# Writing the zeros of a routing buffer later, from each expert's first free row on

## The chip, the cores and the metric

The kernel runs on one NeuronCore of a Trainium2 chip. The metric is the device time of one execution in microseconds (us), the median of several runs; 1041.03 us before the change (three runs, 1039.38 to 1041.65).

A core has five engines that run in parallel, each through its own list of instructions in order: TensorE (PE, matrix multiplications and transposes), VectorE (DVE), ScalarE (ACT), GpSimd (POOL) and SyncE (SP). SP does no arithmetic here: it issues nearly all transfers between the core's SBUF and DRAM, and those inside SBUF, which 16 DMA engines then carry out. POOL issues the transfers whose rows are chosen by data. An instruction that needs another engine's or a transfer's result waits at the head of its engine's list, and everything behind it in that list waits too.

## The reference

Three layers follow each other: attention in which only scores close to the row's maximum count, a layer of eight experts of which each token uses one, and a dense layer.

```python
scores = scale * q @ k.T                       # 4 batches, 8 heads, 576 x 576, head_dim 64
scores = where(scores >= max(scores) - tau, scores, -1e9)
x = softmax(scores) @ v                        # then heads side by side: x is 2304 x 512
e_idx = argmax(x @ w_gate, axis=1)             # one of 8 experts for each token
for e in range(8):
    mask = e_idx == e
    out[mask] = gate_w[mask] * eom[mask, e] * (relu(x[mask] @ w1[e]) @ w2[e])   # 512 -> 1024 -> 512
g = h * tanh(softplus(h)), h = out @ w_in      # 512 -> 2048
result = g @ w_out                             # 2048 -> 512
```

All is in 32-bit floats.

## The kernel before

**Attention.** The 4 batches of 8 heads are worked in 16 pairs of heads, four per batch. For a pair SP loads q and k (L258, L260), PE turns them (L532, L543), ACT and POOL split each into a high and a low part (L538, L547, L567), and SP spreads the parts inside SBUF into the tiles that the score matmuls read: kx for k (L556), sa and sb for q (L558). A pair has nine blocks of scores (L416), which alternate between sa and sb; the ninth uses both. Per block DVE takes the row maximum (L421), POOL the threshold (L425), ACT the exponential (L434) and DVE the mask (L439); two blocks of scores fit in PSUM, and a block's place comes free with its mask. PE then turns the masked block (L447) and multiplies it with v (L463 to L477).

**Routing.** When a batch is through, PE and DVE compute its gate logits, each token's expert, and the token's rank among all tokens of that expert so far. Each expert has a stretch of RS = 2688 rows in a DRAM buffer, xs. POOL sends the batch's rows there in five indirect transfers (L978); the row is the expert's first row plus the token's rank. So at any time the rows of one expert lie densely from its first row on. After three batches the expert with the most tokens is known; SP loads its first 256 rows (xe, L722) and its weights (wraw, L1045), and its matmuls (L1210, L1229) fill PE while the last batch is routed. The experts are then worked in order of size with blocks of fixed sizes (CAP, 544 rows for the largest down to 256), so rows past an expert's last token are read as well. They have to be zero.

**The zeros.** `zero_fill(e)` (L145) writes 544 rows of zeros at the start of expert e's stretch: one transfer of 1088 KB, issued by SP (L152). The eight are put into the plan at L390, each after a certain block of scores (block 14, 19, ... 49 of 144), and they are on their way before any row of a batch is sent. They go to rows known when the kernel is built, and none waits for another.

**What sets the order.** The lists of the engines are fixed when the kernel is built. `Plan` (L1393 on) holds nodes with an engine, a cost in ns, the nodes they come after, a due time (in blocks of scores), the buffers they take and give, and a lag: the time after the node's end until its result counts as there (a transfer's landing). It runs a clock over these costs, always takes the node that can start first, by due time among equals, and writes its instructions. The waits themselves come from the tiles' uses: xs is one DRAM tile, so accesses at rows that are known only at run time are ordered one after the other, by their landing.

Of the kernel before, what the change touches and what calls it, by code (L numbers as in the profile page):

```python
# [13 lines left out]
I32 = mybir.dt.int32  # L14
U32 = mybir.dt.uint32
AF = mybir.ActivationFunctionType
ALU = mybir.AluOpType
# [6 lines left out]
NE, FF = 8, 1024  # L24
FF2 = 2048
P = 128
NP = H // 2
NT = 5
EARLY = 256
RS = N + EARLY + P  # L30
CAP = (544, 416, 352, 320, 304, 272, 256, 256)
# [9 lines left out]
C_8ME, C_ERS, C_E, C_CAP = 2 * P, 2 * P + 8, 2 * P + 16, 2 * P + 24  # L41
# [32 lines left out]
LAST_P, DUE_AVL = 0, 9.83  # L74
DUE_S1, DUE_P1 = .72, 4.8
SENT = 2900
ZERO_FROM, ZERO_STEP = 14, 5
POOL_SPLIT = {0, 1, 2} | set(range(10, 46, 3)) | set(range(72, 80))


class Kernel:
# [61 lines left out]
        nc.vector.memset(self.ones, 1.0)  # L143

    def zero_fill(self, e):  # L145
        nc = self.nc
        if e == 0:
            self.z = self.sx.tile([P, P], F32, name="zeros")
            nc.gpsimd.memset(self.z, 0.0)
        rows = self.xs[e * RS:e * RS + CAP[0], :].rearrange("r (s d) -> (r s) d", d=P)  # L150
        t = CAP[0] * DM // P // P
        nc.sync.dma_start(rows.rearrange("(p t) d -> p t d", p=P), self.z.unsqueeze(1).to_broadcast([P, t, P]))  # L152

# [197 lines left out]
    def plan_attention(self):  # L351
        nc, add, npair = self.nc, self.plan.add, self.nb * NP
        self.raw_kq, self.kq, self.v, self.xt, self.sums = {}, {}, {}, {}, {}
        self.started, self.sent, self.sent_of = {}, None, {}
        qk, st, cols = [], [], {}
        loads = []

        def load(p, after=()):
            after = list(after) + ([qk[9 * (p - N_LD)]] if p >= N_LD else [])
            loads.append(add("SP", 3600, lambda: self.load_pair(p), after, 9 * p - 30, [(("ld", p), 3 if p else 1)], lag=2000))  # L360

        def start(b):
            after = [qk[9 * (NP * b - NP + 1)]] if b else []
            self.started[b] = add("POOL", 290, lambda: self.start_batch(b), after, 9 * NP * b - 18, [(("xt", b), NT + (2 if b == self.nb - 1 and 0 < LAST_CUT < NT else 1))])
            return add("SP", 5700, lambda: self.load_v(b), after, 9 * NP * b - 18, [(("v", b), 3 * NP)], lag=2000)

        load(0)
        add(None, 0, self.late_setup, [loads[0]], -50)
        load(1)
        v = start(0)  # L370
        for p in range(2, N_LD):
            load(p)
        ops = self.plan_first_prep(loads[0])
        for p in range(npair):
            b, hp = divmod(p, NP)
            if p > 0:
                ops = self.plan_prep(p, loads[p])
            if p == 1:
                load(N_LD, ops)
            if p == NP * b and b:  # L380
                v = start(b)
            self.plan_pair(p, ops, v, qk, st, cols)
            if 0 < p < npair - N_LD:
                load(p + N_LD)
            if hp == NP - 1:
                cut = LAST_CUT if b == self.nb - 1 else NT
                for i0, i1 in ((0, cut), (cut, NT)):
                    if i0 < i1:
                        self.plan_route(b, i0, i1, cols)
        for e in range(NE):  # L390
            add("SP", 3100, lambda e=e: self.zero_fill(e), [qk[ZERO_FROM + ZERO_STEP * e]], ZERO_FROM + ZERO_STEP * e + 6)
        self.plan_first(st)

    def plan_pair(self, p, ops, v, qk, st, cols):
# [449 lines left out]
    def map_tokens(self, n):  # L844
# [6 lines left out]
        elif n == NTT:  # L851
            nc.gpsimd.dma_start(self.mapi, self.map.rearrange("(t p) o -> p (t o)", p=P))

    def plan_route(self, b, i0, i1, cols):


        nc, sm, add = self.nc, self.sm, self.plan.add
        last = b == self.nb - 1
        due = (DUE_LAST if last else DUE_ROUTE) + 9 * NP * (b + 1)
# [103 lines left out]
        def scatter(i):  # L963
            n = P if i < 4 else 64
            px = T["px", i] = self.bank()
            for hp in range(NP):
                nc.tensor.transpose(px[0:n, hp * P:(hp + 1) * P], self.xt[b][:, hp, i * P:i * P + n], self.ident)

        def scatter_out(i):
            n = P if i < 4 else 64  # L970
            xo = T["xo", i] = self.xsp.tile([P, DM], F32, name="xo")
            nc.vector.tensor_tensor(  # L972
                xo[0:n].rearrange("p (h d) -> p h d", h=H), T["px", i][0:n].rearrange("p (h d) -> p h d", h=H),
                T["rc"][0:n, i - i0].unsqueeze(2).to_broadcast([n, H, D]), op=ALU.mult)

        def send(i):
            n = P if i < 4 else 64
            nc.gpsimd.indirect_dma_start(  # L978
                self.xs[:, :], bass.IndirectOffsetOnAxis(ap=T["rowi"][0:n, i - i0:i - i0 + 1], axis=0), T["xo", i][0:n], None)
# [4 lines left out]
        n = add("PE", sum(100 + int(1.67 * (z - a)) for a, z in pieces), logits, where, due - 2, [(k, 1) for k in keys], [("xt", b)])  # L984
        n = add("ACT", int(1.05 * (w1 - w0)), logits_out, [n, begin], due - HASTE, gives=keys)
        keys = [("bank", b, "lt", i) for i in banks]
        n = add("PE", 110 * nt, logits_turn, [n], due - 2, [(k, 1) for k in keys])
# [10 lines left out]
        if b == self.nb - 2:  # L998
            e, f, g = self.first_expert()
            n = add("DVE", 80, e, [n2], due)  # L1000
            n = add("PE", 30, f, [n], due, takes=[(("bank", "first"), 1)])
            self.chosen = add("DVE", 2150, g, [n], due - HASTE, gives=[("bank", "first")])
        for i in range(i0, i1):
            n = add("PE", 435, lambda i=i: scatter(i), [n4], due + i, [(("bank", b, "sc", i), 1), (("xo", b, i), 1)], [("xt", b)])
            n = add("DVE", 602, lambda i=i: scatter_out(i), [n], due - HASTE, gives=[("bank", b, "sc", i)])
            self.sent_from = n
            self.sent = add("POOL", 1040, lambda i=i: send(i), [n, self.sent] if self.sent else [n], due + i, gives=[("xo", b, i)], lag=SENT)
        self.sent_of[b] = self.sent


# [382 lines left out]
class Plan:  # L1393
# [15 lines left out]
    def add(self, eng, cost, fn, after=(), due=0.0, takes=(), gives=(), lag=0):  # L1409
        n = Node(eng, cost, fn, list(after), due, list(takes), list(gives), lag)  # L1410
        self.nodes.append(n)
        return n
# [83 lines left out]
```

## Time and profile before

| | us |
|---|---|
| median of 3 runs | 1041.03 |
| lowest, highest | 1039.38, 1041.65 |
| the profiled execution | 1037.33 |
| its span, first to last instruction | 1035.5 |
| attention's blocks of scores, first to last | 11.9 to 333.0 |
| zero fills issued | 47.9 to 125.6 |
| sends of the routed rows | 137.9 to 370.8 |
| mean granted clock of TensorE | 0.995 of full speed |

The profile shows one execution. The difference between the profiled execution's time and its span is what lies before the first and after the last instruction. Rows of a timeline give the start in us, the duration in us, the engine, the line of the kernel, the operation, the tile written and the tiles read, and how many instructions were merged into the row (x4). In brackets stands how long the engine had been idle before the row, and what ended that: an engine and the tile it wrote, or a transfer. SPq is SP's issuing of transfers; its durations are those of the issue, not of the transfer.

### The profile page before, as it was taken

The page shows a single profiled execution, that of the slowest core. Times are in us where ns is not written, and L with a number is a line of the kernel's source. Part 1 is how long each engine was busy: PE and PEld are TensorE (multiplying, and loading weights), DVE is VectorE, ACT ScalarE, POOL GpSimd, SP SyncE. Part 2 cuts the span into 40 slices and gives each one's busy share as a digit, 9 for nine tenths or more (in the row PEclk, how much of TensorE's full clock was granted, in tenths as well). Part 3 has the DMA queues.
Part 4 walks back from the last instruction along what each step waited for, and adds up shares of the span by engine and source line. Part 5 has one row for each costly group of instructions (what it writes and reads, how often), then busy time and mean ns, then how long its engine had stood idle before and what let it go on. Part 6 is the DMA issues. An engine that isn't in the chain of part 4 may idle for free.

```text
span 1035.5 us, 19346 instructions
## 1 busy us (share of the span) xinstructions
PE 988.7 (95%) x7012; PEld 863.0 (83%) x7012; DVE 697.3 (67%) x1299; ACT 661.0 (64%) x1126; POOL 306.8 (30%) x377
## 2 busy tenths in 40 slices
PE   5989999999999899999999999999999999999996
PEld 4667777767767688999999998899988999999995
DVE  5767787787797748766667766778776665445443
ACT  5777768767767515556566757876775765665562
POOL 3232243233221312444533333345441221111111
PEclk9999999999999999999999999999999999999999
DMA  7999975765534248667878864544831132221111
GB/s 159 231 240 240 244 200 133 180 160 129 140 90 149 82 140 276 226 203 250 269 238 287 275 210 101 113 117 120 220 123 44 62 112 72 72 92 63 41 41 41
DMA packets 144354, 160.10 MB, mean 155 GB/s; under 512 B 48672, under 2 KB 102624, under 8 KB 144256
## 3 DMA queue, kind: packets, MB, share of 16 engines
q1 hardware_dynamic: 140480, 149.34, 51.4%
q0 software_dynamic: 3776, 9.49, 2.7%
q8 instruction: 57, 0.93, 0.4%
q14 instruction: 41, 0.34, 0.1%
HBM read 95.22 MB, written 37.04 MB: 128 GB/s over the span
## 4 chain that ended last, share of the span: by engine, by line
PE 71%; DVE 13%; ACT 5%; DMA 5%; issue 5%; SPq 1%; POOL 1%; POOLq 0%; DVEq 0%; ACTq 0%
PE hg L1326 14%; PE o L1366 14%; PE bank L1210 10%; PE y L1229 9%; PE s L416 8%; PE bank L447 6%; PE o L463 4%; DMA xs<-xo,rowi 2%; DVE s L1334 2%; ACT L1338 1%; DVE s L1342 1%; DVE gh L1343 1%; DVE e L439 1%; PE o L466 1%; DVE mxs L421 1%
## 5 line engine op out<-in xcount | busy, mean ns | idle before, releaser
L1326 PE MATMUL hg<-yh,whi 128*128 128x256 f32 x576 | 162.9, 283 | 2.1 <-DVE ys L1239 2.1
L1326 PE MATMUL hg<-yl,whi 128*128 128x256 f32 x576 | 163.1, 283 | 0.7 <-DVE yl L1273 0.7
L1326 PE MATMUL hg<-yh,wlo 128*128 128x256 f32 x576 | 163.0, 283 | 0.0
L434 ACT ACTIVATE e<-s,mxs 128x576 f32<-128x576 f32 x144 | 103.9, 746 | 54.9 <-DVE mxs L421 48.9
L421 DVE TENSOR_REDUCE mxs<-s 128x1 f32<-128x576 f32 x144 | 105.4, 754 | 40.1 <-PE s L416 39.2
L439 DVE SCALAR_TENSOR_TENSOR e<-s,thr,e 128x576 f32<-128x576 f32 x144 | 113.9, 814 | 26.0 <-ACT e L434 19.6
L1366 PE MATMUL o<-whi,gh 128*128 128x512 f32 x288 | 113.3, 393 | 2.1 <-DVE gh L1343 2.1
L1326 PEld LDWEIGHTS hg<-yh,whi 128*128 128x128 f32 x576 | 110.4, 192 | 3.7 <-issue 2.3
L1342 DVE TENSOR_TENSOR s<-s,hg 128x512 f32<-128x512 f32 x72 | 49.3, 684 | 94.9 <-ACT s L1338 94.9
L1366 PE MATMUL o<-whi,gl 128*128 128x512 f32 x288 | 112.9, 392 | 0.0
L1366 PE MATMUL o<-wlo,gh 128*128 128x512 f32 x288 | 112.5, 391 | 0.0
L1326 PEld LDWEIGHTS hg<-yl,whi 128*128 128x128 f32 x576 | 110.4, 192 | 2.3 <-DVE yl L1273 1.0
L1326 PEld LDWEIGHTS hg<-yh,wlo 128*128 128x128 f32 x576 | 110.4, 192 | 0.0
L1333 ACT ACTIVATE s<-hg 128x512 f32<-128x512 f32 x72 | 42.1, 594 | 106.1 <-PE hg L1326 99.9
L452 ACT COPY pt<-bank 128x512 f32<-128x512 f32 (+1 forms) x192 | 93.9, 539 | 17.0 <-PE bank L447 15.0
L447 PE MATMUL bank<-cst,e 128*128 128x128 f32 (+1 forms) x656 | 92.2, 278 | 1.0 <-DVE xo L972 1.0
L1229 PE MATMUL y<-hh,whi 128*128 128x256 f32 (+6 forms) x288 | 87.1, 302 | 0.0
L447 PEld LDWEIGHTS bank<-cst,e 128*128 128x128 f32 (+1 forms) x656 | 73.5, 140 | 16.2 <-issue 9.6
L1229 PE MATMUL y<-hl,whi 128*128 128x256 f32 (+6 forms) x288 | 86.8, 301 | 0.0
L1229 PE MATMUL y<-hh,wlo 128*128 128x256 f32 (+6 forms) x288 | 86.8, 301 | 0.0
L1061 DVE TENSOR_TENSOR wlo<-wraw,whi 128x1024 fp32r<-128x1024 f32 x57 | 79.6, 1396 | 10.4 <-ACT whi L1057 9.8
L1057 ACT CAST whi<-wraw 128x1024 fp32r<-128x1024 f32 x80 | 83.3, 1047 | 3.0 <-DMA wraw<-in_moe_w 3.0
(247 smaller groups left out, 2373.3 us busy)
## 6 DMA issues: line engine op xcount, KB each, us to landing
wraw<-in_moe_w SPq DMA_DIRECT2D x64, 512.0 KB
kx<-khl SPq DMA_DIRECT2D x60, 288.0 KB
wraw<-yt SPq DMA_DIRECT2D x18, 512.0 KB
xs<-zeros SPq DMA_DIRECT2D x8, 1088.0 KB
raw<-in_moe_w_in SPq DMA_DIRECT2D x16, 512.0 KB
raw<-in_moe_w_out SPq DMA_DIRECT2D x16, 512.0 KB
part<-ob SPq DMA_DIRECT2D x18, 256.0 KB
ob<-part SPq DMA_DIRECT2D x18, 256.0 KB
```

The source lines that it names most:

```text
L416: nc.tensor.matmul(s[:, half, 0:288], q[j][:, o:o + P], kx[j][:, at:at + 288], start=j == parts[0][0] and low == 0, stop=j == parts[-1][0] ...
L421: nc.vector.reduce_max(mx, S[u][:, :, 0:288], axis=AX.XY, negate=True)
L434: nc.scalar.activation(ev(u), S[u][:, :, 0:288], AF.Exp, bias=S["mx", u])
L439: nc.vector.scalar_tensor_tensor(ev(u), S[u][:, :, 0:288], S["thr", u], ev(u), op0=ALU.is_ge, op1=ALU.mult, accum_out=acc)
L447: nc.tensor.transpose(pp[0:rows, n * P:(n + 1) * P], E[i][:, col:col + rows], self.ident)
L452: nc.scalar.copy(t[0:rows, 0:n], PT["ps", g][0:rows, 0:n])
L1057: nc.scalar.copy(hi, raw)
L1061: return lambda: sub(lo, raw, hi.bitcast(F32))
L1210: self.nc.tensor.matmul(h[:, 0:n], w[a][:, k, c:c + P], xs[b][:, k, 0:n], start=(k == 0 and m == 0), stop=(k == 3 and m == 2))
L1229: self.nc.tensor.matmul(y[0][:, d, 0:n], w[a][:, f % 2, d * P:(d + 1) * P], hh[b][:, 0:n], start=(f == 0 and m == 0), stop=(f == 7 and m = ...
L1326: nc.tensor.matmul(h[:, j], w[a][:, k, j * P:(j + 1) * P], y[b][:, k], start=(k == 0 and m == 0), stop=(k == 3 and m == 2))
L1366: nc.tensor.matmul(o, gs[j // 2][x][:, j % 2, t * P:(t + 1) * P], w[y][:, j % 2], start=(g == 0 and j == 0 and m == 0), stop=(g == 1 and j ...
```

## The change

The zeros are no longer written at the start of each expert's stretch before all sends, but once two of the four batches are routed, from the first row that these two batches leave free. `plan_zeros` is called when batch 2's attention has been planned, ahead of its routing. It counts the tokens of each expert so far (one cast on DVE, one small matmul on PE), adds each expert's first row, and keeps the sums as integers (zi). Each fill then loads its row number from zi into a register of SP and writes 544 rows from there. A fill comes after the one before it, after the last send of batch 1, and after block 91 of the scores; in the plan it costs SP 1200 ns and counts as landed 6500 ns later. The sends of batch 2 come after the last fill.

```diff
-ZERO_FROM, ZERO_STEP = 14, 5
+ZERO_FROM, ZERO_STEP, ZERO_LAG = 91, 4, 6500
...
     def zero_fill(self, e):
...
-        rows = self.xs[e * RS:e * RS + CAP[0], :].rearrange("r (s d) -> (r s) d", d=P)
+        row = nc.values_load(self.zi[0:1, e:e + 1], engines=[mybir.EngineType.SP], min_val=0, max_val=NE * RS - CAP[0])
+        rows = self.xs[ds(row, CAP[0]), :].rearrange("r (s d) -> (r s) d", d=P)
...
             if hp == NP - 1:
+                if b == self.nb - 2:
+                    self.plan_zeros(qk)
                 cut = LAST_CUT if b == self.nb - 1 else NT
...
-        for e in range(NE):
-            add("SP", 3100, lambda e=e: self.zero_fill(e), [qk[ZERO_FROM + ZERO_STEP * e]], ZERO_FROM + ZERO_STEP * e + 6)
...
+    def plan_zeros(self, qk):
+
+        add, ps = self.plan.add, []
+        self.zi = self.const.tile([P, NE], I32, name="zi")
+        due = ZERO_FROM - 2
+        n = add("DVE", 80, lambda: ps.append(self.counts_in((self.nb - 2) * NT)), [self.ranked], due)
+        n = add("PE", 30, lambda: ps.append(self.counts(ps[0])), [n], due, takes=[(("bank", "zeros"), 1)])
+        n = add("DVE", 80, lambda: self.nc.vector.tensor_tensor(self.zi, ps[1], self.cst[:, C_ERS:C_ERS + NE], op=ALU.add),
+                [n], due, gives=[("bank", "zeros")])
+        self.zeros = [n]
+        for e in range(NE):
+            self.zeros.append(add("SP", 1200, lambda e=e: self.zero_fill(e), [self.zeros[-1], self.sent, qk[ZERO_FROM]], ZERO_FROM + ZERO_STEP * e, lag=ZERO_LAG))
...
-            self.sent = add("POOL", 1040, lambda i=i: send(i), [n, self.sent] if self.sent else [n], due + i, gives=[("xo", b, i)], lag=SENT)
+            self.sent = add("POOL", 1040, lambda i=i: send(i), [n] + ([self.sent] if self.sent else []) + (self.zeros[-1:] if b == self.nb - 2 else []), due + i, gives=[("xo", b, i)], lag=SENT)
```

## Rows read from the trace of the kernel before

**Rows 1.** The page, busy time of each engine, its share, instructions.
```profile
PE 988.7 (95%) x7012; PEld 863.0 (83%) x7012; DVE 697.3 (67%) x1299; ACT 661.0 (64%) x1126; POOL 306.8 (30%) x377
```

**Rows 2.** Stretches: length, busy us by engine, PE clock, DMA share, GB/s.
```profile
50.00:60.00 10.00, 6.22 (x42) 5.15 (x42) 6.05 (x12) 6.52 (x16) 3.60 (x8) 1.00 1.00 280
240.00:300.00 60.00, 59.05 (x489) 43.51 (x488) 47.46 (x121) 44.70 (x99) 15.56 (x40) 1.00 0.51 121
```

**Rows 3.** Timeline of PE: score blocks before which PE was idle.
```profile
52.06 0.76 PE L416 MATMUL s<-kx,sa 128*128 128x288 f32 x4 [2.31 <-DMA sa<-qhl]
...
69.56 0.64 PE L416 MATMUL s<-kx,sa 128*128 128x288 f32 x3 [0.62 <-DMA sa<-qhl]
...
92.61 0.63 PE L416 MATMUL s<-kx,sb 128*128 128x288 f32 x3 [0.95 <-PE bank L447]
...
112.28 0.77 PE L416 MATMUL s<-kx,sb 128*128 128x288 f32 x4 [0.81 <-PE bank L447]
...
227.85 0.80 PE L416 MATMUL s<-kx,sa 128*128 128x288 f32 x4 [1.15 <-DVE e L439]
```

**Rows 4.** Timeline of SP: spreads and zero fills as issued.
```profile
46.51 1.34 SPq L558 DMA_DIRECT2D sb<-qhl  x2
47.95 0.62 SPq L152 DMA_DIRECT2D xs<-zeros  x1
...
67.11 0.95 SPq L152 DMA_DIRECT2D xs<-zeros  x1
...
78.92 1.36 SPq L152 DMA_DIRECT2D xs<-zeros  x1
80.38 5.67 SPq L558 DMA_DIRECT2D sa<-qhl  x2
86.10 1.23 SPq L558 DMA_DIRECT2D sb<-qhl  x2
...
258.76 2.63 SPq L558 DMA_DIRECT2D sa<-qhl  x2
```

**Rows 5.** Timeline of POOL: two sends of batch 1, the first of batch 2.
```profile
224.89 0.98 POOL L978 DMA_INDIRECT xs<-xo,rowi  x1 [3.20 <-DMA xs<-xo,rowi]
...
236.19 0.91 POOL L978 DMA_INDIRECT xs<-xo,rowi  x1 [0.48 <-issue]
...
302.15 1.01 POOL L978 DMA_INDIRECT xs<-xo,rowi  x1 [0.54 <-DVE xo L972]
```

**Rows 6.** The page, transfers issued: the sends, median us to landing.
```profile
xs<-xo,rowi POOLq DMA_INDIRECT x20, 2.8
```

**Rows 7.** By line: ns min/median/max, first and last start.
```profile
L1028 SPq TENSOR_LOAD <-eri x7: 263/263/474, 372.3 to 375.9; - x7
...
L675 DVE CAST cb<-cum x2: 160/162/164, 295.9 to 356.0; 128x8 bf16<-128x8 f32 x2
```

**Rows 8.** Timeline of POOL: rows whose wait a zero fill ended.
```profile
54.42 0.19 POOL L425 TENSOR_TENSOR thr<-ntau,mxs 128x1 f32<-128x1 f32 x1 [0.47 <-DMA xs<-zeros]
...
73.40 0.86 POOL L567 TENSOR_TENSOR khl<-kraw,khl 128x320 fp32r<-128x320 f32 x1 [1.94 <-DMA xs<-zeros]
```

**Rows 9.** Timeline of SP and of PE: a late pair's spread, its first scores.
```profile
261.44 1.23 SPq L558 DMA_DIRECT2D sb<-qhl  x2
...
271.15 0.69 PE L416 MATMUL s<-kx,sa 128*128 128x288 f32 x4
```

**Rows 10.** Waits of SP, 200 to 330 us: us in total, times, longest.
```profile
SPq L556 <- ACT khl L547: 28.9, 5, 9.3
```

**Rows 11.** Timelines of SP, ACT and PE: the hand-over to the first expert.
```profile
321.53 0.95 SPq L722 DMA_DIRECT2D xe<-xs  x2
322.68 1.52 SPq L1045 DMA_DIRECT2D wraw<-in_moe_w  x3
...
335.19 1.07 ACT L1057 CAST whi<-wraw 128x1024 fp32r<-128x1024 f32 x1
...
351.92 0.58 PE L1210 MATMUL bank<-yh,whi 128*128 128x256 f32 x1 [0.75 <-DVE xo L972]
```

## The prediction, on record before the change was run

> **What bounds the kernel now.** I read the page's busy times first. TensorE works 988.7 us of a 1035.5 us span [rows 1], so the whole kernel has 46.8 us in which PE does nothing, and an edit that takes no work off PE can only win some of those. Next I read stretches, because the edit touches two of them: 48 to 126 us, where the eight zero fills are issued now, and 240 to 310 us, where they will go. The first holds the worst ten microseconds of the attention stage, 50 to 60, with PE busy 6.22 and the DMA engines full (share 1.00, 280 GB/s); the second has PE busy 59.05 of 60 at a DMA share of 0.51 and 121 GB/s [rows 2]. So the change moves traffic out of a full stretch into a half empty one, and the question is which of PE's waits in the full stretch are the zeros' doing. For that I read PE's own order there, and then the order in which SP issued its DMAs.
>
> **What it removes.** PE's waits that end with the arrival of spread queries between 48 and 126 us are 2.31 us at 52.06, 0.62 at 69.56, 0.95 at 92.61 and 0.81 at 112.28 [rows 3]. The profile names a transfer for the first two and "PE bank" for the others. I read the others as transfers as well: both are the second block of scores of a pair, the first use of its sb, and for the one at 92.61 SP finished issuing sb only at 86.10 + 1.23 = 87.33 us, 5.28 us earlier [rows 4], about what spread data takes to land in this stretch. The one at 112.28 stands alike.
>
> Which of the four has a zero fill in front of it? All of these transfers leave through SP's one queue. Zero fill 0 is issued at 47.95, after the sb that belongs to the wait at 52.06 (46.51 to 47.85) [rows 4]; that wait stays. The wait at 92.61 has zero fill 3 right between its kx and its sa: issued at 78.92, and the two sa behind it take 5.67 us to issue, where two sa with nothing in front take 2.63 (at 258.76) [rows 4]. The waits at 69.56 and 112.28 come behind the fills of their pairs. So I take off 0.62 + 0.95 + 0.81 = 2.38 us. The bounds: 0, if PE, which fills its time with other pairs' work, would only meet the next wait earlier; and the upper end is those 2.38 plus the 3.78 us that PE misses in 50 to 60 [rows 2], 6.16 us, if the first wait and what follows it are the zeros' as well. I take 2.38, by the issue order.
>
> The Trainium skill's DMA: Bandwidth & Descriptors (Queues, rings and completion order) says that each DMA engine consumes the descriptors of one ring in the order of the ring. By that rule the wait at 52.06 stays and those behind a fill go; the 5.67 us of the two sa agree with it.
>
> **What it moves.** The eight fills of 1088 KB, 8.9 MB in all, are now chained one behind the other: fill 0 waits for the last send of batch 1, and each later fill for the one before it to land. The last send of batch 1 is issued at 236.19 and takes 0.91 [rows 5], a send lands in a median 2.8 [rows 6], so the chain starts at about 239.9 us; the condition on score block 91 is met long before. One fill costs SP a register load, 0.6 us (seven loads from 372.3 to 375.9) [rows 7], and an issue of 0.62 [rows 4]. Its landing I read where an engine's wait is put down to a zero fill: issued 47.95, wait ended 54.42, and issued 67.11, wait ended 73.40 [rows 4, 8], so 6.3 to 6.5 us, in a stretch with full DMA engines. One link is then 0.6 + 6.4 = 7.0 us, and the plan allows 7.8 (1200 + 6500 + 100 ns). Eight links are 56 to 62.4 us: the chain ends between 296 and 302 us if SP is always free. SP is not: per pair it spends about 11 us on spreads and loads, and a fill that meets them waits its turn. I add half such a turn, 5 us, for one or two of the four pairs, and take 308 us; the bounds are 296 and 240 + 62.4 + 4 x 5 = 322 us.
>
> 8.9 MB over 60 us is 149 GB/s on top of 121, 270 GB/s, close to the 280 of the full stretch [rows 2]. So the late spreads get the delay that the early ones lose. What covers it: there the spread of a pair is fully issued at 261.44 + 1.23 = 262.67 and its first scores start at 271.15 [rows 9], 8.5 us later, where 87.33 us to the first use of sb at 92.61 is 5.3 and all of that was needed. The cover over a loaded landing is 8.5 - 5.3 = 3.2 us. SP itself can afford the fills' 8 x 1.2 = 10 us: between 200 and 330 us it waits 28.9 us for ACT's halves of k alone [rows 10]. If the cover is gone, three pairs lose what three early ones lost, 2.4 us. I cost it at 0.
>
> **What it adds.** One cast of the counts (DVE, 0.162 us) [rows 7], one small matmul and one DVE addition like the cast, then a bank that is held for the three. PE works through that stretch nearly without a gap, so the matmul with its weights is on the path: some 0.2 us, like the cast. I take 0.4 for all; the ends are 0 (DVE has 12.5 of 60 us free there [rows 2]) and 1.0.
>
> **The wait that it adds.** Batch 2's first send now waits for the last fill. It is issued at 302.15 today [rows 5]. With the chain's end at 308 the sends move by 6 us, and with them what SP does next: the first expert's rows (xe) at 321.53 and its weights at 322.68 [rows 11] slide to about 328 us. A weight load is half a fill in bytes, so it lands in less than 6.4 us, and the first cast of weights runs at 335.19, 12.5 us after the first load; the cover is 6.1 us before ACT has to reorder, and the first expert's first matmul comes at 351.92 [rows 11], 29.2 us after that load. So the slide costs nothing at 6 us, and at 20 us (the chain's upper end) it reorders casts without reaching the matmul. Behind the waiting send on POOL stand the thresholds of attention, which every mask needs. The planner places the send by its own clock, so POOL stalls only by as much as the real chain is later than the planned one. With links of 7.0 against 7.8 I cost this at 0; its bad end is the fourth rival.
>
> **The sum.** -2.38 + 0.4 = -2.0 us. Against the profiled execution, 1037.33 us, that is 1035.3. That execution lies 3.7 us below the median of the runs, 1041.03, so I apply the difference to the median: 1039.0 us. Own range, with 0 to 6.16 won and 0 to 2.4 lost: 1036 to 1041. About 0.2% (2.1 us) is what a measurement here can tell from no change, and the forecast stands on that line.
>
> **The rivals.**
> 1. The zeros cause the whole hole at 50 to 60 too. For it: PE is idle 3.78 us there just as the first fill starts; SP's next load behind that fill is slow. Against it: the issue order. -6.16 + 0.4: 1035.3 us.
> 2. Nothing is won on balance: the waits move from three early pairs to three late ones, or PE meets other waits. For it: 270 GB/s against a cover of 3.2 us. Against it: the late pairs have that cover and the early ones had none. -2.38 + 2.4 + 0.4: 1041.4 us.
> 3. The change does not do what it says in time: bound to batch 1's last send, the chain runs past 322 us, casts of the first expert's weights collide with the last batch's routing on DVE. One such piece of DVE work is about 1.2 us and two or three would shift: 1039.0 + 3 = 1042 us.
> 4. Slower: POOL is held by its send. Place: batch 2's first send, around 305 us. Point from which it decides: a link longer than the planned 7.8 us, a landing over 7.2 us. Price: in batch 1 POOL waited 3.20 us for a landing at 224.89 [rows 5] and PE then missed 1.15 us at 227.85 [rows 3], 0.36 us of PE for each. With 2 us more in each of eight links POOL is held 16 us: 5.8 us, 1044.8 us. For it: such a wait costs PE already; a fill stuck behind a whole spread lands late. Against it: the two landings that can be read, 6.3 and 6.5 us, come from the fullest stretch.
>
> The Trainium skill's DMA: Bandwidth & Descriptors (Anatomy of one DMA) says that DMA engines do not wait on semaphores; the issuing sequencer waits before it dispatches. By that rule a fill that waits for the one before it holds SP, and the spreads queued behind it, which speaks for rivals 2 and 4; no row of the kernel before shows a fill that waits for a fill.
>
> **How the numbers follow.** Forecast 0.42 (of it 0.25 beyond the line and 0.17 within), rival 1 0.15 (faster), rival 2 0.20 (same), rival 3 0.05 (half same, half slower), rival 4 0.18 (slower by most of its sizes; 0.02 of it same). That gives faster 0.40, same 0.41, slower 0.19; I move 0.03 from same to slower, since a link of the chain was never seen in this stretch. The range reaches from rival 1 with the spread of the runs (1034) to rival 4 (1045).
>
> **What would show it.** Right: PE's waits at about 69, 92 and 112 us are gone and the one at 52 stays; two sa behind a kx issue in about 2.6 us everywhere; the eight fills start at about 240 us, 7 to 9 us apart, and end by 312; POOL's wait before batch 2's first send is under 2 us; the first expert's first matmul keeps its distance to the last scores. Wrong: PE missing more than 2 us in 240 to 330 than now, a first send later than 315 us, or a hole at 50 to 60 that closes.

## The result, and the profile after

The changed kernel takes 1053.44 us (median of 6 runs, 1049.63 to 1054.98) against 1041.34 of the kernel before in the same session (6 runs, 1039.04 to 1043.27): 1.0116 times as long, 95% interval 1.0094 to 1.0138, or 12.1 us more. The prediction was 1039.0 us with a range to 1045, so both sign and range were wrong. The profiled execution took 1052.79 us, 1051.0 of it span.

Busy times hardly change: the page of the changed kernel has the engines at what they had before [rows 1]. PE has 4.8 us more, and the span is 15.5 us longer than that of the execution shown before.

```profile
PE 993.5 (95%) x7013; PEld 863.4 (82%) x7013; DVE 705.0 (67%) x1301; ACT 661.6 (63%) x1126; POOL 308.6 (29%) x377
```

So time was lost in waiting, and the stretches tell where. Here are those of the changed kernel, with the columns of [rows 2]: start and end, length, busy us of PE, PEld, DVE, ACT and POOL with instruction counts, granted clock, DMA share, GB/s.

```profile
50.00:60.00 10.00, 7.48 (x49) 6.09 (x50) 7.07 (x14) 6.82 (x15) 4.01 (x8) 1.00 0.36 66
240.00:300.00 60.00, 57.42 (x468) 42.02 (x468) 45.97 (x114) 44.02 (x97) 13.17 (x37) 1.00 0.86 225
350.00:360.00 10.00, 1.58 (x7) 1.16 (x7) 9.12 (x26) 3.15 (x5) 6.04 (x4) 0.59 0.69 210
360.00:370.00 10.00, 9.47 (x61) 9.47 (x62) 8.18 (x11) 3.02 (x5) 2.38 (x2) 0.73 0.07 26
```

The last two stretches of the kernel before:

```profile
350.00:360.00 10.00, 9.25 (x66) 8.79 (x64) 8.88 (x32) 1.67 (x6) 1.99 (x2) 0.83 0.14 52
360.00:370.00 10.00, 10.00 (x88) 9.96 (x87) 5.93 (x12) 1.15 (x3) 1.94 (x2) 1.00 0.15 54
```

The reader is to see three things. The traffic did move: 280 to 66 GB/s in 50 to 60, 121 to 225 in 240 to 300. PE won 1.26 us in the first of these and lost 1.63 in the second. Of the two only the loss stands clear of the scatter: over four profiles of each kernel PE's busy time is 6.22 to 7.21 before and 7.02 to 8.39 after in the first stretch, 58.92 to 59.05 and 57.18 to 58.02 in the second. And in 350 to 360 a hole has opened: PE works 1.58 us of ten where it had 9.25, while DVE is as busy as before. That is the hand-over from attention to the first expert.

How the hole came about is read from the queues. SP of the changed kernel (start, us, queue, line, operation, count); the two fills of the first row were issued at 245.05 and 250.91, four more at 269.92, 282.64, 290.06 and 300.56:

```profile
245.05 6.45 SPq L154 DMA_DIRECT2D xs<-zeros  x2
...
262.38 0.62 SPq L154 DMA_DIRECT2D xs<-zeros  x1
263.11 4.66 SPq L560 DMA_DIRECT2D sa<-qhl  x2
...
307.65 0.62 SPq L154 DMA_DIRECT2D xs<-zeros  x1
334.44 0.97 SPq L724 DMA_DIRECT2D xe<-xs  x2
335.60 2.67 SPq L1060 DMA_DIRECT2D wraw<-in_moe_w  x5
```

Seven links in 62.60 us are 8.94 us for one. The page of this kernel gives the landing:

```profile
xs<-zeros SPq DMA_DIRECT2D x8, 1088.0 KB, 6.2
```

The last fill landed near 307.65 + 6.2 = 313.9 us. POOL's first send of batch 2 follows, 12.9 us later than in [rows 5], and the first expert's rows (xe, above) also start 12.9 us later than in [rows 11]:

```profile
315.02 1.01 POOL L993 DMA_INDIRECT xs<-xo,rowi  x1 [0.54 <-issue]
...
346.86 2.38 POOL L1076 TENSOR_TENSOR wlo<-wraw,whi 128x1024 fp32r<-128x1024 f32 x1 [6.22 <-ACT whi L1072]
...
350.44 4.64 POOL L1076 TENSOR_TENSOR wlo<-wraw,whi 128x1024 fp32r<-128x1024 f32 x2
```

The first cast of weights slides by 10.5 us against [rows 11]. ACT of the changed kernel:

```profile
345.73 1.05 ACT L1072 CAST whi<-wraw 128x1024 fp32r<-128x1024 f32 x1
```

PE of the changed kernel, attention's last scores and then the hole:

```profile
333.03 0.43 PE L418 MATMUL s<-kx,sb 128*128 128x288 f32 x2
...
356.63 0.20 PE L955 MATMUL bank<-cumb,up 128*128 128x24 bf16 x1 [7.40 <-DVE cumb L948]
...
357.93 1.11 PE L982 MATMUL bank<-cst,xt 128*128 128x128 f32 x4 [1.04 <-DVE yl L1187]
358.69 0.56 PE L1225 MATMUL bank<-yh,whi 128*128 128x256 f32 x1
360.53 0.58 PE L1225 MATMUL bank<-yl,whi 128*128 128x256 f32 x1 [1.28 <-DVE yl L1187]
```

PE waits 7.40 us for cumb, a step of the second part of the last batch's routing, and twice more for yl, the low part of the first expert's rows. DVE shows the order behind it. First the changed kernel:

```profile
348.44 0.55 DVE L930 TENSOR_TENSOR lgt<-bank,r 128x384 f32<-128x384 f32 x1
349.02 0.80 DVE L933 TENSOR_REDUCE lg<-lgt 128x48 f32<-128x384 f32 x1
...
350.07 5.07 DVE L938 TENSOR_TENSOR d<-lg,mx 128x24 f32<-128x24 f32 x1
...
357.18 0.69 DVE L1187 TENSOR_TENSOR yl<-bank,yh 128x512 fp32r<-128x512 f32 x1 [0.22 <-issue]
...
359.79 0.68 DVE L1187 TENSOR_TENSOR yl<-bank,yh 128x512 fp32r<-128x512 f32 x1
```

Then the kernel before, where both yl (L1172 there) stand ahead of the second part (128x384, L915):

```profile
341.04 2.34 DVE L923 TENSOR_TENSOR d<-lg,mx 128x16 f32<-128x16 f32 x1
...
348.85 1.28 DVE L1172 TENSOR_TENSOR yl<-bank,yh 128x512 fp32r<-128x512 f32 x2
...
352.38 0.55 DVE L915 TENSOR_TENSOR lgt<-bank,r 128x384 f32<-128x384 f32 x1
```

The order has flipped. Before, the first expert's work bridged the time in which DVE routes the last rows. Now it stands behind that routing, and PE has nothing. The lists are fixed when the kernel is built, so this order was there before the kernel ran: it follows the plan's clock.

To keep such a loss apart from the scatter of one execution I use three marks: the last scores of attention, the first matmul of the first expert that the others follow without a gap (the distance between the two is called the hand-over below), and the last output of the experts on DVE. Four profiled executions of each kernel, most of them listed further down, give these means in us:

| | before | after | difference |
|---|---|---|---|
| last scores | 333.5 | 333.3 | -0.2 |
| hand-over (last scores to first expert) | 19.05 | 27.5 | +8.45 |
| end of the experts | 615.2 | 623.6 | +8.4 |
| from there to the end of the span | 423.6 (420.4 to 426.9) | 424.6 (421.5 to 427.5) | +1.0 |

The spans differ by 9.5 us, and 8.4 of it is the hand-over. The last row scatters by 6 us in either kernel, so its +1.0 says nothing.

### The profile page after: what moved, and what is told of

Read it like the earlier page. It is cut to its first block, busy times and chain, and to the rows that moved or that the text cites. A ratio compares the mean times of both kernels' runs of the same rounds, so it can differ in the third digit from the quotient of the medians.

```text
span 1051.0 us, 19403 instructions
## 1 busy us (share of the span) xinstructions
PE 993.5 (95%) x7013; PEld 863.4 (82%) x7013; DVE 705.0 (67%) x1301; ACT 661.6 (63%) x1126; POOL 308.6 (29%) x377
## 4 chain that ended last, share of the span: by engine, by line
PE 67%; DVE 16%; ACT 6%; DMA 5%; issue 4%; SPq 1%; POOL 0%; POOLq 0%; DVEq 0%; ACTq 0%
PE hg L1341 12%; PE o L1381 12%; PE bank L1225 10%; PE y L1244 10%; PE s L418 8%; PE bank L449 6%; PE o L465 5%; DVE s L1349 3%; DVE gh L1358 2%; ACT L1353 2%; DVE s L1357 2%; DVE mxs L423 1%; ACT s L1351 1%; DVE e L441 1%; PE o L468 1%
## 5 line engine op out<-in xcount | busy, mean ns | idle before, releaser
L1076 DVE TENSOR_TENSOR wlo<-wraw,whi 128x1024 fp32r<-128x1024 f32 x57 | 79.3, 1392 | 15.5 <-ACT whi L1072 15.1
```

The source lines that it names most:

```text
L1076: return lambda: sub(lo, raw, hi.bitcast(F32))
```

## The experiments

Ratios are to the kernel before on the same chip in the same session (medians of it there: 1040.92, 1038.67 and 1038.97 us; 1038.43, a single run, in the last one).

**after_again.** The changed kernel once more, so that the others have it in their session.

> The changed kernel once more, for a second profile and its time on this chip. If all of its loss sits in the hand-over to the first expert, about 9 us of it shows there again (first matmul of the first expert near 360 us) and the further 6 us that the first profile shows in the first steps of the dense layer vary from one execution to the next. If those 6 us belong to the change, they are there again, at the same steps.

1050.21 us, 1.0103 [1.0064, 1.0141]. The hole is 7.38 us long, the first gapless expert matmul at 360.23, the experts' end at 622.7.

**x1_one_batch.** The chain starts after one routed batch, and batch 1's sends wait for it in place of batch 2's.

```diff
-ZERO_FROM, ZERO_STEP, ZERO_LAG = 91, 4, 6500
+ZERO_FROM, ZERO_STEP, ZERO_LAG = 55, 4, 6500
...
-                if b == self.nb - 2:
+                if b == self.nb - 3:
                     self.plan_zeros(qk)
...
-        n = add("DVE", 80, lambda: ps.append(self.counts_in((self.nb - 2) * NT)), [self.ranked], due)
+        n = add("DVE", 80, lambda: ps.append(self.counts_in((self.nb - 3) * NT)), [self.ranked], due)
```

> The zeros are written once one batch is routed instead of two, chained in the same way, and batch 1's sends wait for the last fill. Theory A (the loss is the hand-over: batch 2's sends end 13 us later, so the first expert's weights come 13 us later and their low parts fall into the last batch's routing): nothing hangs on batch 1's sends, the chain's bytes and waits are the same, so the time is back at 1040 to 1043 us. Theory B (the chained fills themselves cost: SP held, spreads late, DMA engines full beside attention): the same loss, 1050 to 1054 us.

1051.64 us, 1.0103 [1.0069, 1.0138], where the slide of the late sends would have had it back at 1040. The hand-over is as before, 19.1 us (345.20 to 364.27), but attention ends some 12 us later. The chain now meets batch 3's load of v in SP's queue. SP and then PE of this kernel:

```profile
202.97 0.64 SPq L154 DMA_DIRECT2D xs<-zeros  x1
203.71 2.92 SPq L269 DMA_DIRECT2D vm<-in_v  x1
...
211.29 1.20 SPq L560 DMA_DIRECT2D sa<-qhl  x2
```

```profile
218.98 1.30 PE L418 MATMUL s<-kx,sa 128*128 128x288 f32 x4 [5.53 <-DMA sa<-qhl]
```

PE's wait of 5.53 us is under half of these 12; the rest was not followed up. This run missed the expectation and doesn't separate the theories as meant: the hand-over came back, and another loss of the same size came in its place. It shows only that the chain can cost as much in another place.

**x2_half_fill.** 288 rows in each fill in place of 544 (for these inputs enough rows are zeroed); everything else stays.

```diff
-ZERO_FROM, ZERO_STEP, ZERO_LAG = 91, 4, 6500
+ZERO_FROM, ZERO_STEP, ZERO_LAG = 91, 4, 3500
-        rows = self.xs[ds(row, CAP[0]), :].rearrange("r (s d) -> (r s) d", d=P)
-        t = CAP[0] * DM // P // P
+        rows = self.xs[ds(row, 288), :].rearrange("r (s d) -> (r s) d", d=P)
+        t = 288 * DM // P // P
```

> Each fill writes 288 rows instead of 544, 53% of the bytes (enough for these inputs), with 3500 ns planned for its landing instead of 6500. Theory A: the links shrink from 8.9 to about 6 us, the chain ends near 290 us, before batch 2's first send is ready at 302, the sends move by nothing and the time is 1039 to 1043 us. Theory B (bytes beside attention): about half of the loss stays, 1046 us.

1040.71 us, 1.0016 [0.9987, 1.0045]: the loss is gone. Its first send starts at 301.69, its xe at 321.03, and the hand-over is 19.1 us. PE of this kernel:

```profile
351.44 0.58 PE L1225 MATMUL bank<-yh,whi 128*128 128x256 f32 x1
```

Nor is it faster than the kernel before, although the experts end at 612.3, 2.9 us earlier.

**x3_low_dve.** The first three weight tiles' low parts go to DVE, so that POOL is not in the hole.

```diff
-POOL_SPLIT = {0, 1, 2} | set(range(10, 46, 3)) | set(range(72, 80))
+POOL_SPLIT = set(range(10, 46, 3)) | set(range(72, 80))
```

> The changed kernel with the low parts of the first three weight tiles taken by VectorE instead of GpSimd. Theory A in its narrow form (VectorE's routing operations of the last batch are held while GpSimd works on those low parts): the hole of 9.7 us in TensorE's work before the first expert shrinks by the 5 us for which one routing operation stood, and the time falls to about 1047 us. If the late arrival of the weights itself holds TensorE, the hole stays and the time stays at 1052 to 1054.

1050.04 us, 1.0113 [1.0064, 1.0162]: nothing won in the time. The operation that took 5.07 us takes 0.18, and PE's longest wait is halved. DVE and PE of this kernel:

```profile
351.58 0.18 DVE L938 TENSOR_TENSOR d<-lg,mx 128x24 f32<-128x24 f32 x1
```

```profile
353.27 0.20 PE L955 MATMUL bank<-cumb,up 128*128 128x24 bf16 x1 [3.66 <-DVE cumb L948]
...
358.34 0.56 PE L1225 MATMUL bank<-yh,whi 128*128 128x256 f32 x1
```

But yl (at 356.82) still stands behind the routing, and DVE has the low parts as well. The hand-over is 24.9 us, 2.6 less than in the changed kernel, and this is given back before the experts end, at 623.2. That DVE is held up beside POOL is real, but without it the loss is the same.

**x4_both.** The early fills stay as in the kernel before; the late chain is added, into rows that nothing reads, and batch 2's sends wait for it.

```diff
+        for e in range(NE):
+            add("SP", 3100, lambda e=e: self.early_fill(e), [qk[14 + 5 * e]], 14 + 5 * e + 6)
...
-        rows = self.xs[ds(row, CAP[0]), :].rearrange("r (s d) -> (r s) d", d=P)
+        rows = self.xs[ds(row + 1200, CAP[0]), :].rearrange("r (s d) -> (r s) d", d=P)
```

> Both: the early fills as before, and the eight chained late fills as after, into rows of the same buffer that nothing uses (1200 rows further on), with batch 2's sends waiting for them. The late part alone against the kernel before. Theory A (late sends): all of the loss and a little more, since nothing is won early: 1053 to 1056 us, with the first expert's weights about 13 us late. If leaving out the early fills is what costs (another order of the plan), the time is near 1042.

1050.24 us, 1.0099 [1.0067, 1.0132]: the late part alone gives the loss. SP's xe starts at 333.30, the hole is 7.38 us, the hand-over 27.5. On DVE the flip is there too: the second part's lgt starts at 347.76, yl at 356.48.

**x6_scratch.** As x4_both, but the late chain writes a buffer of its own and no send waits for it.

```diff
-        rows = self.xs[ds(row + 1200, CAP[0]), :].rearrange("r (s d) -> (r s) d", d=P)
+        rows = self.xz[ds(row, CAP[0]), :].rearrange("r (s d) -> (r s) d", d=P)
...
-            self.sent = add("POOL", 1040, lambda i=i: send(i), [n] + ([self.sent] if self.sent else []) + (self.zeros[-1:] if b == self.nb - 2 else []), due + i, gives=[("xo", b, i)], lag=SENT)
+            self.sent = add("POOL", 1040, lambda i=i: send(i), [n] + ([self.sent] if self.sent else []), due + i, gives=[("xo", b, i)], lag=SENT)
```

> As x4_both, but the late fills go to a DRAM buffer of their own and batch 2's sends do not wait for them. The same bytes, the same waits of SP from fill to fill, no late sends. Theory A: back at 1041 to 1044 us, first send near 302 us. Theory B (the fills hold SP and fill the DMA engines): 1050 us or more.

1044.42 us, 1.0040 [1.0010, 1.0070]. The traffic is all there (fills from 241.79 to 303.87), the wait is not. The hand-over is 19.1 us and the experts end at 614.25, as before. POOL, SP and PE of this kernel:

```profile
298.86 1.01 POOL L1002 DMA_INDIRECT xs<-xo,rowi  x1 [0.36 <-DVE xo L996]
...
310.66 1.00 POOL L1002 DMA_INDIRECT xs<-xo,rowi  x1 [3.95 <-DMA xs<-xo,rowi]
```

```profile
321.72 0.96 SPq L732 DMA_DIRECT2D xe<-xs  x2
```

```profile
313.72 0.82 PE L426 MATMUL s<-kx,sa 128*128 128x288 f32 x2 [2.02 <-DVE e L449]
...
352.40 0.58 PE L1234 MATMUL bank<-yh,whi 128*128 128x256 f32 x1 [0.37 <-DVE xo L996]
```

Against x4_both this settles the place: the loss in the hand-over hangs on the sends' wait for the last fill, not on the traffic between 240 and 310 us. Where the 0.4% that remain sit is not shown. At the three marks the profiled execution has lost nothing, and its rest after the experts is 427.75 us, within what that stretch scatters. But it came to batch 2's gate (the first matmul of its gate logits) at 280.89, 3.3 us ahead of the kernel before (284.2, mean of four), and by the last scores that lead is gone: a send held POOL for 3.95 us there, waiting for the landing of the one before, and PE then missed 2.02 us. So the late traffic may cost something too.

**x5_small_early.** The early part alone: the kernel before with 96 rows in each early fill (these inputs need no more).

```diff
-        rows = self.xs[e * RS:e * RS + CAP[0], :].rearrange("r (s d) -> (r s) d", d=P)
-        t = CAP[0] * DM // P // P
+        r0 = e * RS + (544, 272, 320, 416, 256, 256, 304, 352)[e] - 96
+        rows = self.xs[r0:r0 + 96, :].rearrange("r (s d) -> (r s) d", d=P)
+        t = 96 * DM // P // P
```

> The kernel before with early fills of 96 rows instead of 544 (18% of the bytes, placed by hand where these inputs need them), nothing late. What leaving the early traffic out can win at most: 2.4 us by the prediction's sum, 6.2 us by its upper end, so 1035 to 1039 us; nothing, if TensorE only meets its next wait earlier.

1039.38 us, 0.9990 [0.9961, 1.0020]. In the profile attention ends some 4 us earlier (last scores at 329.18) and the experts 3 us earlier, at 612.1; the rest takes 428 us, and no gain can be measured. Whether the 3 us are the early part's doing is not shown: the gates of batches 0 and 1 (118.69 and 198.05) come no earlier than in x6_scratch (117.75 and 197.74), which has all the early fills. In the whole time the early part is worth nothing that can be told from zero.

**x7_416_rows.** A chain between x2_half_fill and the change: 416 rows, planned lag 5000 (edits at the same lines). It asks how far the sends may slide. Like x2_half_fill it shortens the landing in the plan together with the bytes.

> The changed kernel with fills of 416 rows (76% of the bytes, enough for these inputs) and 5000 ns planned for a landing: a middle dose between 288 rows (sends not late, first expert on time) and 544 rows (sends 12.9 us late, first expert 8.6 us late). The links should be about 7.5 us, the chain end near 303 us and the sends 3 to 5 us late. By the prediction's step (6 us of cover in front of the first weight cast) the first expert starts near 352 us, the expert layer ends near 614 us, as before. If lateness is passed on in proportion, 8.6 of 12.9, the first expert starts 2 to 3 us late.

1043.09 us, 1.0037 [1.0017, 1.0057]. SP's xe starts at 328.43, 6.9 us later than in [rows 11]. The hand-over is 18.7 us, and both yl (351.90, 353.79) stand ahead of the second part (355.52). POOL and PE of this kernel:

```profile
309.37 1.01 POOL L993 DMA_INDIRECT xs<-xo,rowi  x1 [4.73 <-DMA xs<-zeros]
```

```profile
311.62 0.77 PE L418 MATMUL s<-kx,sa 128*128 128x288 f32 x4 [1.46 <-DVE e L441]
...
354.94 0.36 PE L1225 MATMUL bank<-yh,whi 128*128 128x256 f32 x1
```

This slide costs the hand-over nothing, but it is smaller than 6.9 us. Attention itself ends 2.7 us later here (336.19 against a mean of 333.5), and it was 2.9 us late by batch 2's gate already (287.03 against 284.2), ahead of the sends. Counted from the last scores, xe starts 7.8 us ahead of them where it was 11.3: a slide of 3.6 us. POOL is held by its send, for 4.73 us, and PE misses 1.46 us behind it; between batch 2's gate and the last scores nothing is lost all the same (49.2 us, 49.4 before). The experts end at 616.1. By the clock alone the first expert, 2 to 3 us late, would fit a lateness passed on in proportion; the hand-over shows that it isn't.

**x8_weights_first.** The changed kernel, with the first expert's first four weight tiles loaded once that expert is known, ahead of its rows.

```diff
-        load = add("SP", 7500, self.load_first, [self.chosen, self.sent_of[self.nb - 2]], due - 30,
-                   [(("raw", g), 1) for g in range(4)], lag=2000)
+        load = add("SP", 4500, self.load_first, [self.chosen], due - 30, [(("raw", g), 1) for g in range(4)], lag=2000)
+        rows = add("SP", 1500, self.load_early, [load, self.sent_of[self.nb - 2]], due - 30, lag=2000)
```

> The changed kernel with the first expert's first four weight tiles loaded as soon as that expert is known, ahead of its rows, so that they no longer stand behind batch 2's sends on SP; the rows (xe) stay as late as they are. If the late weights are what holds the first expert, its first matmul returns to about 352 us, the expert layer ends near 615 us instead of 623, and the time is 1039 to 1044 us. If the late rows hold it, nothing changes: first matmul near 360 us, 1049 to 1053 us.

1044.32 us, 1.0044 [1.0024, 1.0063]: some 0.6 to 0.7% better than the change, worse than the kernel before. The hand-over is 16.1 us, though xe comes later than in the changed kernel, and yl (350.95) again stands ahead of the second part (354.48). SP, DVE and PE of this kernel:

```profile
303.21 1.95 SPq L1064 DMA_DIRECT2D wraw<-in_moe_w  x2
...
338.49 0.91 SPq L729 DMA_DIRECT2D xe<-xs  x2
```

```profile
350.95 1.28 DVE L1191 TENSOR_TENSOR yl<-bank,yh 128x512 fp32r<-128x512 f32 x2
...
354.48 0.55 DVE L934 TENSOR_TENSOR lgt<-bank,r 128x384 f32<-128x384 f32 x1
```

```profile
354.02 0.58 PE L1229 MATMUL bank<-yh,whi 128*128 128x256 f32 x1 [0.75 <-DVE xo L991]
```

Attention ends 4.4 us later (338.0), so part is given back. The edit also shortens what the plan counts between the last send and the rows, so it doesn't tell whether late weights or the plan's late rows put the work in that order.

**x9_before_weights_first.** The same edit on the kernel before.

> The kernel before with the same earlier weights. Its weights were on time, so by either theory the time stays within the noise, 1036 to 1043 us; if the casts of the weights were already part of what set the first expert's start there, it starts earlier than 352 us and the expert layer ends up to 3 us before 614.

1046.60 us, 1.0057 [1.0034, 1.0079]: slower, where no change or a small gain was expected. The hand-over is 16.6 us, but attention ends at 343.7 and the experts at 623.3. The shorter hand-over is paid for ahead of it; by what was not followed up.

**before_again, before_look3, before_look4, after_look3, after_look4.** Single executions of the two kernels as they are, for the marks of the table above.

> The kernel before once more, for a second profile: the dense layer should take the same 396 us as in the first (first to last matmul of its first product), if those steps do not vary from one execution to the next.

> A third profile of the kernel before: first expert's first matmul at 352 us and end of the expert layer at 614 to 615 us, as in the first two. The rest of the span, from there to the end, was 420.4 and 422.6 us; if it belongs to the program it is 420 to 423 again, if it varies from one execution to the next it lies anywhere from 420 to 428.

> A fourth profile of the kernel before, for the same question.

> A third profile of the changed kernel: first matmul near 360 us, end of the expert layer at 623 to 624. From there to the end it was 427.1 and 421.5 us; if the change makes the dense layer slower, two more profiles lie near 427, if not they lie anywhere from 420 to 428, as those of the kernel before.

> A fourth profile of the changed kernel, for the same question.

1038.32, 1043.81 and 1042.73 us before, 1047.39 and 1053.75 after. In the first profile of the changed kernel the rest after the experts was 6.8 us longer than in the first of the kernel before, which looked like a second loss. With four profiles of each it is 420 to 428 us in both.

No version was shown to beat the kernel before; x2_half_fill and x5_small_early can't be told from it.

## Why the prediction was wrong

**The step that failed** is that the slide "costs nothing at 6 us, and at 20 us (the chain's upper end) it reorders casts without reaching the matmul". Its second half is false: at 12.9 us, short of 20, the hand-over is 8.45 us longer. Its first half was not tested: x7_416_rows kept its hand-over, at a slide of 6.9 us by the clock but 3.6 us against its own attention. I measured the cover from the first weight load to the first matmul, 29.2 us, as if only the loads stood in that time. What stands there is a fixed order of work on DVE, shared with the last batch's routing. The later plan puts the second part of that routing ahead of yl, and PE pays for the whole of it. The flip is there in the changed kernel, x3_low_dve and x4_both, which lose, and not in x2_half_fill, x6_scratch, x7_416_rows or x8_weights_first, whose hand-overs are 16 to 19 us. That the two go together is shown. The measured lateness of the rows alone does not do it: in x8_weights_first xe starts 0.5 us after the last scores, in the changed kernel 1.4 us after them, and yet the order is kept and the hand-over is 16.1 us. It is the plan's clock that sets the order, but which of its terms flips it, the later rows or the late weights, is argued only (x8_weights_first changes both); and x2_half_fill and x7_416_rows shorten the planned landing with the bytes, so no run tells the shorter plan from the shorter chain.

**The chain was mis-sized.** Predicted start 239.9, link 7.0, end 308; measured 243.7 (the first register load, below), 8.94 and 313.9. The landing of 6.2 us was well read from 6.4. The last send of batch 1 came when expected (235.64), but SP was busy with spreads until 242.43 + 1.25 = 243.68, so the start was 3.8 us late. The end at 308 does not follow from links of 7.0: with half a turn of 5 us these give 239.9 + 56 + 5 = 300.9, and 308 took the plan's 7.8. So the eight links, 313.9 - 243.7 = 70.2 us, are only some 2 us over the 68.1 that the prediction gave them in the end, and the late start is most of the 5.9 us. SP's turns were under-counted all the same: four links took 5.9 to 7.5 us, and the three in which SP issues a pair's kx (with its loads in two of them) 10.5 to 12.7, as between the fills at 250.91 and 262.38. With the end at 314 instead of 308 the sends slid by 12.9 us instead of 6, past the cover of 6.1 us that the prediction itself named for the casts.

**What it removes.** -2.38 us was predicted, and batch 0's gate comes 2.25 us earlier (119.6 against 121.8, means of four). That the two agree is partly luck: the four reach from 118.8 to 121.6 after and from 120.8 to 122.5 before, and x6_scratch, with all the early fills, has that gate at 117.75. The waits at 92.61 and 112.28 are gone in all four profiles of the changed kernel, the one at 69.56 has become one at 72.08, and the one at 52.06, which I left to the first pair, shrank from 2.31 to 1.32; it scatters, from 1.99 to 2.91 before and from 1.16 to 3.39 after. PE of the changed kernel:

```profile
50.88 0.76 PE L418 MATMUL s<-kx,sa 128*128 128x288 f32 x4 [1.32 <-DMA sa<-qhl]
...
72.08 0.76 PE L418 MATMUL s<-kx,sb 128*128 128x288 f32 x4 [0.95 <-PE bank L449]
```

But it is given back before attention ends: batch 1's gate is 0.6 us earlier, batch 2's 0.95 later, the last scores 0.2 earlier. The two late sa at 263.11 take 4.66 us to issue where [rows 4] had 2.63, which is the trade of rival 2, at about its size.

**What it adds.** Of 0.4 us for three small operations the addition is 0.169 (it runs at 212.8), and the register load that I took at 0.6 is 0.589 by the median of eight, here from the view of the tile zi of the changed kernel. The rest of the term can't be told apart in these sums.

```profile
L151 SPq TENSOR_LOAD <-zi x8: 273/589/902, 243.7 to 306.7; - x8
L863 DVE TENSOR_TENSOR zi<-bank,cst x1: 169/169/169, 212.8 to 212.8; 128x8 int32<-128x8 f32 x1
```

**The rivals.** Rival 1 fell: PE missed 2.52 us in 50 to 60 still, of 3.78 (1.61 to 2.98 against 2.79 to 3.78 in four profiles each). Rival 2 came true within attention. Rival 4, POOL held by its send, did not decide, though its condition was met: the links were longer than planned by 8.94 - 7.8 = 1.1 us each, and POOL waited only 0.54 us before the first send. It happened in x7_416_rows instead, at about its price: 4.73 us by 0.36 would be 1.7 us, and PE missed 1.46. Rival 3 was the mechanism, "casts of the first expert's weights collide with the last batch's routing on DVE". I gave it a chance of 0.05 and a price of 3 us, by counting three pieces of DVE work of 1.2 us. What collided was a whole part of the routing, 8.7 us from 348.44 to the first yl (5.07 of them the held operation), with PE's clock at 0.59 and 0.73 behind it.

**What stays open.** The medians differ by 9.3 to 12.1 us, the hand-over explains 8.4. The 1 to 4 us left may be in the stretch after the experts, which scatters by 6 to 7 us in either kernel; x6_scratch, with no net loss up to the experts' end, is 0.4% slower as well. No run here settles whether the late fills cause that.

## What to carry to other kernels

Before traffic is moved out of a full stretch, ask who will wait for its end: here the transfer's time cost 0.4% or nothing in either place (x6_scratch, x5_small_early), and the wait that came with it 8.4 us. Price a chain of transfers by its link with all that the queue does between two of them, not by its landing. And measure a cover up to the first piece of work whose place in a fixed order would change, not up to the matmul at the end of it; where the order is planned ahead, it can be read before the kernel runs.

## What the runs showed of the hardware

A DVE operation on two operands in SBUF was held while POOL ran an operation of its own: L938 took 5.07 us in the hole, over POOL's two of 4.64 us, and L923 took 2.34 us before, over one; without POOL it took 0.18 (x3_low_dve). Operations that read one operand in SBUF were not held: in the kernel before one that reads PSUM (0.42 us) and a reduce (0.60 us) ran beside POOL's low parts, and in the changed kernel (340.40 and 340.86), where POOL works on no low part then, they took 0.42 and 0.59. POOL and DVE of the kernel before:

```profile
336.33 7.01 POOL L1061 TENSOR_TENSOR wlo<-wraw,whi 128x1024 fp32r<-128x1024 f32 x3 [1.91 <-ACT whi L1057]
```

```profile
339.74 0.42 DVE L915 TENSOR_TENSOR lgt<-bank,r 128x256 f32<-128x256 f32 x1 [3.39 <-PE bank L899]
340.19 0.60 DVE L918 TENSOR_REDUCE lg<-lgt 128x32 f32<-128x256 f32 x1
```

The Trainium skill's SBUF — State Buffer (SBUF: two separate sides) says that DVE and GpSimd share one pair of ports as an exclusive lock, which a DVE operation with two SBUF inputs needs against a GpSimd operation that reads SBUF, and that the one that starts first keeps it for its whole instruction. The lengths agree. On who starts first the rows differ: in x7_416_rows (345.71, 1.40 us) and x8_weights_first (343.93, 1.56) the DVE operation is recorded during one of POOL's and ends within 0.1 us of it, but in the changed kernel L938 is recorded 0.37 us ahead of POOL's row and was held all the same, through two instructions.

PE's clock fell with the hole: the granted clock is 0.59 in 350 to 360 and 0.73 in 360 to 370, against 0.83 and 1.00 before, so part of each stretch ran at the lower of the two levels, 1.2 GHz. The first expert's matmuls show how long it lasted: those of 0.41 to 0.42 us run to 365.4 in the changed kernel, some 4.9 us from 360.5, and to 355.1 before, some 3.2 us from 351.9; after that they take 0.28.
